# Retention followed by a low-rank mixer on one core: some of batch 1's transposes moved from TensorE to DMA, and batch 2's loads reordered

## The chip, the cores and the metric

The kernel runs on one core of a Trainium2 chip. Five engines share the work: TensorE (PE; its weight loads are listed as PEld), VectorE (DVE), ScalarE (ACT), GpSimd (POOL) and SyncE (SP), which here only issues DMA transfers. Each engine executes its own instructions in program order and waits on semaphores for the others. The metric is the device time of one execution in microseconds (us); lower is better.

## What is computed

Inputs are q, k and v of shape (4, 8, 768, 64): batch, heads, sequence, head dimension. First a linear attention with a decay per head, then a mixer on its output:

```python
gamma = 1.0 - 2.0 ** (-5.0 - np.arange(H))          # one decay per head
for t in range(S):
    state = gamma * state + k[:, :, t] (outer) v[:, :, t]
    y[:, :, t] = q[:, :, t] @ state / sqrt(D)
x = y with heads side by side                       # (4, 768, 512)
h = x.transpose(0, 2, 1) @ U @ V                    # rank 32 along the sequence
u = x + h.transpose(0, 2, 1)
out = u + relu(u @ w_ch1) @ w_ch2                   # 512 -> 2048 -> 512
```

## The kernel before, in words

The sequence of 768 is cut into six chunks of 128 (`NCK = 6`). Within a chunk the attention is two matrix products with a mask between them; between chunks a state is carried. Per chunk and batch:

- **load** (L137, or `load_heads`, L106): one 128x512 float32 tile each of k, q and v, 256 KB, issued by SyncE into a ring of 20 tiles. L137 moves rows of 64 numbers (256 bytes), L106 rows of 128 (512 bytes).
- **prep** (L207; `prep_q1` for batch 1's q): a cast or a multiplication with the decays to bf16, mostly on GpSimd, into `kd`, `qd` (called `qp` for batch 1) and `vd`. It frees a ring tile.
- **turn**: k and q are needed transposed (`kT`, `qT`). For batches 2 and 3 `turn_chunk` (L245) has SyncE issue two DMA transposes a chunk. For batch 1 `turn_k1` and `turn_q1` (L252, L261) do it on TensorE with matmuls against the identity, into a PSUM bank, and ACT or DVE copies the result out. Batch 0 has a code of its own and isn't touched.
- **score** (L276): k^T q into PSUM (matmuls of L281), then the mask (DVE, L284).
- **mix** (L289): state times query, scores times values, x copied out by ACT, the next state.

Then the low-rank part makes u (`lr_expand`, addition on DVE at L351) and its transpose `uT`. For the first four chunks of batch 1 `lr_proj_turn` and `lr_uT` make it on TensorE. The remaining u chunks go through `lr_turn` (L356): matmuls against the identity for batches 0 and 1, DMA transposes from SyncE (L359) for batches 2 and 3.

The mixer of a batch is a list of 48 pieces of nearly equal cost: 16 "up" pieces of four matmuls 128x512 (L429) on the first 512 positions, 8 "up" pieces of eight matmuls 128x256 (L442) on the other 256, and 24 "down" pieces of four matmuls (L458), four to an output row block of 128. In batch 3 the last row block is cut by columns, 384 and 128. The output is added to u on DVE (L465). It is put into a list of `stores`, from which GpSimd issues one (L408) after the next piece; only the 128-column part of the very last row block is issued by SyncE at once (L468).

**What sets the order.** The program is written out in one order, and each engine's queue follows it. `weave` (L483) goes through the 48 pieces of batch b and inserts the attention steps of batch b+1 between them. Each step has a mark, a fraction of the batch's total cost of 48 x 0.864 = 41.47; it is inserted ahead of the first piece whose accumulated cost has reached the mark. The tables `AT` and `LR` hold the marks: for batch 1 the starts of the three chunk pairs; for batches 2 and 3 the first pair's start and the distance of the pairs (`step`); then the delay of the mixes after their pair (`dm`) and the lead of the turns ahead of it (`dt`). A mark of 1.27 lies in batch 1's pieces at 0.27.

**When loads are issued.** `feed` is the list of loads in order: batch 1's by pairs, then batches 2 and 3 chunk by chunk. `feed_more` (L128) issues loads as long as fewer than `n_open` are issued and fewer than 20 ring tiles are held; each prep calls it. Before the change `n_open` is 6 * NCK = 36, so batch 2's loads follow batch 1's as ring tiles come free. `open_chunk` raises `n_open` by 3, one chunk; in batch 1's pieces six marks, 0.25 + 0.1 ci, open batch 3's chunks.

SyncE's queue is a single one: loads, DMA transposes and the last store all pass through it in program order. An instruction whose operand isn't ready holds up what stands behind it. The compiled program also makes each of its transfers wait for the eighth transfer before it. TensorE's queue is as strict: a score that waits for `kT` or `qT` holds up the mixer's matmuls behind it.

Of the kernel before, what the change touches and what calls it, by code (L numbers as in the profile page):

```python
# [10 lines left out]
bf16 = mybir.dt.bfloat16  # L11
# [5 lines left out]
def kernel(  # L17
# [11 lines left out]
    nc = tc.nc  # L29
    P = 128  # L30
    B, H, S, D = q.shape
    NCK = S // P
# [14 lines left out]
    rpre = ctx.enter_context(tc.tile_pool(name="rpre", bufs=4))  # L47
# [78 lines left out]
    n_fed, n_held, n_open = [0], [0], [6 * NCK]  # L126

    def feed_more(t=None):  # L128
        while n_fed[0] < n_open[0] and n_held[0] < RING:
            nm, b, ci = key = feed[n_fed[0]]  # L130
            n_fed[0] += 1
            n_held[0] += 1
            ready[key] = t = ring() if t is None else t
            if (nm, b) == ("q", 1):
                load_heads(t, q, 1, ci % 2, ci // 2)
            else:
                nc.sync.dma_start(  # L137
                    out=t.rearrange("p (h d) -> p h d", h=H),
                    in_=src_of[nm][b, :, ts(ci, P), :].rearrange("h p d -> p h d"))
            t = None  # L140
# [51 lines left out]
    pre = {}  # L192
# [12 lines left out]
        feed_more()  # L205

    def prep(nm, b, ci, eng="P"):  # L207
        if (nm, b) == ("q", 1):
            return prep_q1(ci)
        src = ready.pop((nm, b, ci)).rearrange("p (h d) -> p h d", h=H)  # L210
        t = rpre.tile([P, H, D], bf16, tag=nm + "d", name=f"{nm}d_{b}_{ci}")
        g = {"k": None, "q": gq, "v": gk}[nm]
        if g is not None:
            g = g[:, ci, :, None].to_broadcast([P, H, D])
        cast(eng, t, src, g)
        pre[nm, b, ci] = t
        n_held[0] -= 1
        feed_more()
# [21 lines left out]
    bts = {}  # L240

    def open_x(b):
        xs[b] = xp.tile([P, NCK, DM], bf16, tag="x", name=f"x_{b}")

    def turn_chunk(b, ci):  # L245
        for nm in "kq":
            t = bts[nm, b, ci] = rpre.tile([P, 4, P], bf16, tag=nm + "T",
                                           name=f"{nm}T_{b}_{ci}", bufs=3)
            nc.sync.dma_start(out=t, in_=pre[nm, b, ci].rearrange("p h d -> p (h d)"),
                              transpose=True)  # L250

    def turn_k1(ci):  # L252
        t = bts["k", 1, ci] = rpre.tile([P, 4, P], bf16, tag="kT", name=f"kT_1_{ci}",
# [100 lines left out]
                v4(xs[b][:, ds(j0, nj), e]), op=ALU.add)  # L354

    def lr_turn(b, j0):  # L356
        if b > 1:
            for j in (j0, j0 + 1):
                nc.sync.dma_start(out=uTs[b][:, :, ts(j, P)], in_=us[b][:, j],  # L359
                                  transpose=True)  # L360
            return
        r = R[j0 // 2 % 2]
        for c in range(NCB):
            for jj in range(2):
                nc.tensor.matmul(r[:, c // 2, ds(256 * (c % 2) + P * jj, P)],
                                 us[b][:, j0 + jj, ts(c, P)], ident, start=True,
                                 stop=True)
        evac("A", uTs[b][:, :, ds(j0 * P, 2 * P)],
             r.rearrange("p n (c t) -> p (n c) t", c=2))
# [40 lines left out]
    def mlp_pieces(b):  # L410
        gT = gtp.tile([P, NM, S], bf16, tag="gT", name=f"gT_{b}")
        pieces = []
        n = [0]

        def relu(dst, src):
            n[0] += 1
            if n[0] % 3 == 0:
                nc.vector.tensor_relu(dst, src)  # L418
            else:
                nc.scalar.activation(dst, src, AF.Relu)  # L420

        def up(m, lo, sz):
            def f():
                g_p = begun.pop((b, m, lo), None)
                c0 = 3 if g_p is not None else 0
                if not c0:
                    g_p = bank("mlp")
                for c in range(c0, NCB):
                    nc.tensor.matmul(g_p[:, :sz], w1b[:, c, ts(m, P)],  # L429
                                     uTs[b][:, c, ds(lo, sz)], start=(c == 0),  # L430
                                     stop=(c == NCB - 1))
                relu(gT[:, m, ds(lo, sz)], g_p[:, :sz])
            return f

        for m in range(NM):
            pieces.append((0.864, up(m, 0, LO)))
        def up_two(m):
            def f():
                g_p = bank("mlp")
                for n in range(2):  # L440
                    for c in range(NCB):
                        nc.tensor.matmul(g_p[:, ts(n, S - LO)], w1b[:, c, ts(m + n, P)],  # L442
                                         uTs[b][:, c, LO:], start=(c == 0),
                                         stop=(c == NCB - 1))
                relu(gT[:, ds(m, 2), LO:], g_p.rearrange("p (n t) -> p n t", n=2))
            return f

        for m in range(0, NM, 2):
            pieces.append((0.864, up_two(m)))
        hold = {}  # L450

        def down(j, m0, n0=0, nn=DM):
            def f():
                if m0 == 0:
                    hold[j, n0] = bank("mlp")
                ch = hold[j, n0]
                for m in range(m0, m0 + 4):
                    nc.tensor.matmul(ch[:, :nn], gT[:, m, ts(j, P)],  # L458
                                     w2b[:, m, ds(n0, nn)],
                                     start=(m == 0), stop=(m == NM - 1))  # L460
                if m0 == NM - 4:
                    o_sb = outp.tile([P, DM], fp32, tag="o_sb",
                                     name=f"o_{b}_{j}_{n0}")[:, :nn]
                    n = ds(n0, nn)
                    nc.vector.tensor_tensor(o_sb, ch[:, :nn], us[b][:, j, n],  # L465
                                            op=ALU.add)
                    if n0:
                        nc.sync.dma_start(out=out[b, ts(j, P), n], in_=o_sb)  # L468
                    else:
                        stores.append((nc.gpsimd, out[b, ts(j, P), n], o_sb))  # L470
            return f

        for j in range(NCK):
            if (b, j) == (B - 1, NCK - 1):
                for n0, nn in ((0, 384), (384, 128)):
                    for m0 in range(0, NM, 4):
                        pieces.append((0.864 * nn / DM, down(j, m0, n0, nn)))
                continue
            for m0 in range(0, NM, 4):
                pieces.append((0.864, down(j, m0)))  # L480
        return pieces
# [18 lines left out]
    def part(f, *args):  # L500
        return lambda: f(*args)
# [267 lines left out]
    load_w1(1024, 512)  # L769
    n_open[0] = 6  # L770
    feed_behind(511)
    n_open[0] = 6 * NCK
    load_w1(1536, 512)
    for j in range(4):
        load_w2(j)
# [3 lines left out]
    for nm in "kqv":  # L779
# [1 line left out]

    AT = {1: ((0.565, 0.685, 0.80), None, (0.045, 0.09), (0.10, 0.045), None),
          2: (0.255, 0.17, (0.05, 0.095), (0.175, 0.11),
              (0.0, 0.085, 0.17, 0.255, 0.34, 0.425)),
          3: (0.20, 0.20, (0.05, 0.095), (0.19, 0.145),
              (-0.07, 0.03, 0.13, 0.23, 0.33, 0.43))}
# [3 lines left out]
    def mark(at, f, *args):  # L792
        marks[int(at)].append((at % 1.0, part(f, *args)))
# [5 lines left out]
    for b in range(1, B):  # L799
        s0, step, dm, dt, at_prep = AT[b]  # L800
        for ci in range(NCK):
            pair_at = b - 1 + (s0[ci // 2] if b == 1 else s0 + step * (ci // 2))
            if b == 1:
                mark(pair_at - dt[0], turn_k1, ci)
                mark(pair_at - dt[1], turn_q1, ci)
            else:
                mark(b - 1 + at_prep[ci], prep_chunk, b, ci)
                mark(pair_at - dt[ci % 2], turn_chunk, b, ci)
            mark(pair_at, score, b, ci)
            mark(pair_at + dm[ci % 2], mix, b, ci)  # L810
            if b > 2:
                mark(b - 2 + 0.25 + 0.1 * ci, open_chunk)
        if b == 1:
            for nm, eng, at in (("k", "AP", (0.51, 0.635)), ("q", "PP", (0.54, 0.67)),
                                ("v", "PP", (0.58, 0.70))):
                for pp in (1, 2):
                    mark(at[pp - 1], prep_two, nm, pp, eng[pp - 1])
            mark(0.905, lr_open, b)
            mark(0.905, lr_proj_turn, b)
            mark(0.94, lr_uT, b)  # L820
            mark(1.11, lr_expand, b, 0, 4)
        else:
            l0, l1, l2, l3 = LR
            mark(b - 1 + l0, mixed, b)
            mark(b - 1 + l1, lr_expand, b, 0, 4)
            mark(b - 1 + l2, lr_turn, b, 0)
            mark(b - 1 + l3, lr_turn, b, 2)
        mark(b + 0.02, lr_expand, b, 4, 2)
        mark(b + 0.08, lr_turn, b, 4)
    mark(0.03, lr_expand, 0, 4, 2)  # L830
    mark(0.10, lr_turn, 0, 4)
    mark(0.16, lr_expand, 0, 0, 4)
# [32 lines left out]
```

## Time and profile before

| | us |
|---|---|
| median of 3 runs | 226.62 (225.92 to 226.64) |
| the profiled execution | 224.54 |
| its span (first to last instruction) | 222.7 |
| TensorE busy | 214.2 (96%) |
| VectorE busy | 96.7 (43%) |
| ScalarE busy | 82.9 (37%) |
| GpSimd busy | 80.0 (36%) |
| DMA queue of SyncE | 23.86 MB, 46.4% of 16 DMA engines' span |
| DMA queue of GpSimd | 10.42 MB, 18.3% |

The page's rows name a line of the kernel, an engine, an operation and its tiles as out<-in. A row of the chain of waits gives the start, the duration and what ran; a row of the timeline gives start, duration, engine, line, operation, tiles and count. "SPq" is SyncE's queue: the duration of its rows is the time in which the instruction holds the queue, with what it waits there; the transfer lands later, and the time from start to landing is asked for separately. In rows by windows the columns are the window and its length, busy time and instructions of PE, PEld, DVE, ACT and POOL, the clock granted to TensorE (1.00 is full), the DMA engines' busy share and GB/s.

Roughly, batch 0's attention fills 0 to 26 us, and the mixers of batches 0 to 3 run from 26 to 78, 78 to 128, 128 to 178 and 178 to 218 us.

### The profile page before, as it was taken

Reading aid. Unit: us, or ns where it says so; the run is one execution under the profiler, and the core shown is the slowest. Engines: PE = TensorE matmul, PEld = TensorE weight load, DVE = VectorE, ACT = ScalarE, POOL = GpSimd, SP = SyncE. Lnnn points to the kernel's source line nnn. Section 1 sums busy time; section 2 is a strip of 40 time slices with the busy share of each in tenths; the row PEclk is TensorE's granted clock in tenths of the full one; section 3 lists DMA queues with packets and bytes.
Section 4 is the critical chain, followed back from the end, with each engine's and each line's share of the span. In section 5 each row is a group of like instructions: output and inputs, shape, how many; then the busy total and the mean of one; then the engine's idle time right before and its main releaser. Section 6 shows DMA issues by size and latency. Waiting matters only on the chain.

```text
span 222.7 us, 4746 instructions
## 1 busy us (share of the span) xinstructions
PE 214.2 (96%) x1955; PEld 122.7 (55%) x1982; DVE 96.7 (43%) x137; ACT 82.9 (37%) x157; POOL 80.0 (36%) x115
## 2 busy tenths in 40 slices
PE   7999999999999999999999999999999999999991
PEld 2567444865665544587444444686544444864451
DVE  6678636235635346625516145251633332222111
ACT  3776454463563244565030044745120144420000
POOL 5588661125750079370101496710111100001010
PEclk9999999999999999999999999999999999999998
DMA  6999999997989996599997644411114330001211
GB/s 175 329 308 243 204 221 200 196 249 172 294 211 259 287 247 138 123 206 203 211 281 185 176 130 96 95 26 24 50 49 150 89 94 0 0 3 47 94 74 68
DMA packets 89301, 34.58 MB, mean 155 GB/s; under 512 B 71216, under 2 KB 87728, under 8 KB 89280
## 3 DMA queue, kind: packets, MB, share of 16 engines
q1 hardware_dynamic: 83152, 23.86, 46.4%
q0 software_dynamic: 6128, 10.42, 18.3%
q8 instruction: 15, 0.25, 0.5%
q14 instruction: 6, 0.05, 0.1%
HBM read 27.46 MB, written 6.29 MB: 152 GB/s over the span
## 4 chain that ended last, share of the span: by engine, by line
PE 56%; issue 31%; POOL 5%; SPq 3%; DMA 2%; DVE 1%; ACT 1%; POOLq 0%; DVEq 0%; ACTq 0%
PE mlp L458 19%; PE mlp L429 17%; PE mlp L442 6%; POOL out_dram L408 3%; SPq L106 2%; DMA in<-in_v_dram 2%; PE r L281 2%; PE r L302 1%; PE st L313 1%; PE r L297 1%; POOL vd L83 1%; PE r L639 1%; PE r L344 1%; PE r L624 1%; PE r L584 1%
## 5 line engine op out<-in xcount | busy, mean ns | idle before, releaser
L458 PE MATMUL mlp<-w2b,gT 128*128 128x512 bf16 (+2 forms) x384 | 86.6, 370 | 1.0 <-issue 0.3
L420 ACT ACTIVATE gT<-mlp 128x512 bf16<-128x512 f32 x64 | 38.1, 597 | 69.9 <-PE mlp L429 57.1
L458 PEld LDWEIGHTS <-gT 128*128 128x128 bf16 x400 | 36.9, 98 | 38.6 <-issue 0.2
L429 PE MATMUL mlp<-uT,w1b 128*128 128x512 bf16 x243 | 56.1, 379 | 0.3
L408 POOL DMA_DIRECT2D out_dram<-o x24 | 13.3, 553 | 105.0 <-DVE o L465 97.3
L418 DVE TENSOR_SCALAR gT<-mlp 128x512 bf16<-128x512 f32 x32 | 22.1, 690 | 46.2 <-PE mlp L429 23.9
L429 PEld LDWEIGHTS <-w1b 128*128 128x128 bf16 x250 | 23.6, 98 | 27.4 <-issue 0.3
L465 DVE TENSOR_TENSOR o<-mlp,u 128x512 f32<-128x512 f32 (+2 forms) x25 | 16.8, 670 | 45.1 <-PE mlp L458 44.4
L442 PE MATMUL mlp<-uT,w1b 128*128 128x256 bf16 x256 | 29.6, 273 | 0.3 <-ACT gT L420 0.2
L442 PEld LDWEIGHTS <-w1b 128*128 128x128 bf16 x256 | 24.7, 98 | 4.2 <-issue 0.4
L284 DVE TENSOR_TENSOR a<-r,mask 128x1024 bf16<-128x1024 f32 x18 | 21.2, 1219 | 7.0 <-PE r L281 7.0
L83 POOL TENSOR_TENSOR vd<-in,gk 128x512 bf16<-128x512 f32 x18 | 18.7, 1040 | 11.8 <-DMA in<-in_v_dram 11.7
L70 ACT ACTIVATE x<-r 128x512 bf16<-128x512 f32 x20 | 11.9, 596 | 26.1 <-PE r L302 25.8
L351 DVE TENSOR_TENSOR u<-r,x 128x512 bf16<-128x512 f32 (+1 forms) x16 | 14.5, 951 | 3.6 <-PE r L344 3.6
L83 POOL TENSOR_TENSOR qd<-in,gq 128x512 bf16<-128x512 f32 x12 | 12.5, 1041 | 0.0
L81 POOL CAST kd<-in 128x512 bf16<-128x512 f32 x16 | 9.7, 611 | 7.3 <-issue 6.2
L70 ACT ACTIVATE nsz<-st 64x256 bf16<-64x256 f32 x30 | 11.2, 372 | 0.3
L83 POOL TENSOR_TENSOR qp<-in,gq 128x512 bf16<-128x512 f32 x6 | 6.2, 1046 | 6.3 <-DMA in<-in_q_dram 6.3
L591 DVE TENSOR_TENSOR a<-r,mask 128x1024 bf16<-128x1024 f32 x6 | 7.3, 1222 | 2.1 <-PE r L584 2.1
L302 PE MATMUL r<-vd,a 128*128 128x64 bf16 x144 | 7.1, 193 | 0.0
L302 PEld LDWEIGHTS <-a 128*128 128x128 bf16 x144 | 6.0, 98 | 0.7
L297 PEld LDWEIGHTS <-qT 128*128 128x128 bf16 x60 | 4.6, 98 | 2.7
(109 smaller groups left out, 151.7 us busy)
## 6 DMA issues: line engine op xcount, KB each, us to landing
in<-in_k_dram SPq DMA_DIRECT2D x24, 256.0 KB, 5.0
in<-in_q_dram SPq DMA_DIRECT2D x24, 256.0 KB, 4.8
in<-in_v_dram SPq DMA_DIRECT2D x24, 256.0 KB, 4.7
out_dram<-o POOLq DMA_DIRECT2D x23, 256.0 KB, 2.5
w1b<-in_moe_w_ch_dram POOLq DMA_DIRECT2D x4, 512.0 KB, 8.1
w2b<-in_moe_w_ch_dram POOLq DMA_DIRECT2D x4, 512.0 KB, 16.1
kT<-kd SPq DMA_TRANSPOSE x12, 2.8
qT<-qd SPq DMA_TRANSPOSE x12, 2.4
```

What stands on the lines that cost most here:

```text
L70: nc.scalar.activation(dst, src, AF.Copy)
L83: e.tensor_tensor(dst, src, scale, op=ALU.mult)
L284: nc.vector.tensor_tensor(a, r.rearrange("p i (n m) -> p i n m", n=4), mask[:, None, None, :].to_broadcast([P, 2, 4, P]), op=ALU.mult)
L302: nc.tensor.matmul(o[:, ts(h, D)], a[:, i, hp], vb[:, h], start=(ci == 0 and h == 0), stop=True, skip_group_check=True)
L351: nc.vector.tensor_tensor(v4(us[b][:, ds(j0, nj), e]), R[g][:, :, :nj * P].rearrange("p c (j e) -> p c j e", j=nj), v4(xs[b][:, ds(j0, nj) ...
L408: eng.dma_start(out=dst, in_=src)
L418: nc.vector.tensor_relu(dst, src)
L420: nc.scalar.activation(dst, src, AF.Relu)
L429: nc.tensor.matmul(g_p[:, :sz], w1b[:, c, ts(m, P)], uTs[b][:, c, ds(lo, sz)], start=(c == 0), stop=(c == NCB - 1))
L442: nc.tensor.matmul(g_p[:, ts(n, S - LO)], w1b[:, c, ts(m + n, P)], uTs[b][:, c, LO:], start=(c == 0), stop=(c == NCB - 1))
L458: nc.tensor.matmul(ch[:, :nn], gT[:, m, ts(j, P)], w2b[:, m, ds(n0, nn)], start=(m == 0), stop=(m == NM - 1))
L465: nc.vector.tensor_tensor(o_sb, ch[:, :nn], us[b][:, j, n], op=ALU.add)
```

## The change

Batch 1's chunks 4 and 5 are no longer transposed by TensorE: `turn_last`, marked at 0.671 of batch 0's pieces, has SyncE issue four DMA transposes for them, k first. Their q is therefore loaded and scaled in the ordinary layout. The same goes for chunks 4 and 5 of batch 1's u: `lr_turn` uses DMA transposes for every batch but 0.

Batch 2's loads are no longer open from the beginning. At first only batch 1's are (`n_open = 3 * NCK`, 18); `turn_last` opens twelve more behind its transposes (chunks 0 to 3 of batch 2), and two `open_chunk` marks in batch 1's pieces add one chunk each.

The marks move: batch 1's last pair from 0.80 to 0.815, its low-rank steps by 0.010 to 0.015, `lr_turn` of its last chunks from 0.08 to 0.055, batch 2's first pair from 0.255 to 0.27 and the pairs' distance from 0.17 to 0.165.

Both column parts of the very last row block are stored by SyncE as soon as they are ready; all other stores go through GpSimd's list as before.

```diff
-            if (nm, b) == ("q", 1):
+            if (nm, b) == ("q", 1) and ci < NCK - 2:
                 load_heads(t, q, 1, ci % 2, ci // 2)
...
-        if (nm, b) == ("q", 1):
+        if (nm, b) == ("q", 1) and ci < NCK - 2:
             return prep_q1(ci)
...
+    def turn_dma(nm, b, ci):
+        t = bts[nm, b, ci] = rpre.tile([P, 4, P], bf16, tag=nm + "T",
+                                       name=f"{nm}T_{b}_{ci}", bufs=3)
+        nc.sync.dma_start(out=t, in_=pre[nm, b, ci].rearrange("p h d -> p (h d)"),
+                          transpose=True)
+
     def turn_chunk(b, ci):
         for nm in "kq":
-            t = bts[nm, b, ci] = rpre.tile([P, 4, P], bf16, tag=nm + "T",
-                                           name=f"{nm}T_{b}_{ci}", bufs=3)
-            nc.sync.dma_start(out=t, in_=pre[nm, b, ci].rearrange("p h d -> p (h d)"),
-                              transpose=True)
+            turn_dma(nm, b, ci)
+
+    def turn_last():
+        for nm in "kq":
+            for ci in (NCK - 2, NCK - 1):
+                turn_dma(nm, 1, ci)
+        n_open[0] = 3 * NCK + 12
+        feed_more()
...
     def lr_turn(b, j0):
-        if b > 1:
+        if b:
...
-                    if n0:
+                    if (b, j) == (B - 1, NCK - 1):
                         nc.sync.dma_start(out=out[b, ts(j, P), n], in_=o_sb)
...
-    n_open[0] = 6 * NCK
+    n_open[0] = 3 * NCK
...
-    AT = {1: ((0.565, 0.685, 0.80), None, (0.045, 0.09), (0.10, 0.045), None),
-          2: (0.255, 0.17, (0.05, 0.095), (0.175, 0.11),
+    AT = {1: ((0.565, 0.685, 0.815), None, (0.045, 0.09), (0.10, 0.045), None),
+          2: (0.27, 0.165, (0.05, 0.095), (0.175, 0.11),
...
             if b == 1:
-                mark(pair_at - dt[0], turn_k1, ci)
-                mark(pair_at - dt[1], turn_q1, ci)
+                if ci < NCK - 2:
+                    mark(pair_at - dt[0], turn_k1, ci)
+                    mark(pair_at - dt[1], turn_q1, ci)
...
+            if b == 2 and ci in (1, 3):
+                mark(pair_at - dt[1] + 0.005, open_chunk)
...
-            mark(0.905, lr_open, b)
-            mark(0.905, lr_proj_turn, b)
-            mark(0.94, lr_uT, b)
+            mark(0.671, turn_last)
+            mark(0.92, lr_open, b)
+            mark(0.92, lr_proj_turn, b)
+            mark(0.95, lr_uT, b)
...
-        mark(b + 0.08, lr_turn, b, 4)
+        mark(b + (0.055 if b == 1 else 0.08), lr_turn, b, 4)
```

## The prediction

> **What bounds the kernel now.** I read first who waits for whom with TensorE (PE) as the waiter. Each line gives waiter, releaser, total us, times, longest:
>
> ```profile
> PE mlp L753 <- DVE zeros L152: 1.2, 1, 1.2
> PE mlp L458 <- issue: 0.3, 2, 0.2
> PE mlp L442 <- ACT gT L420: 0.2, 1, 0.2
> ```
>
> After the start PE waits for nobody worth naming; the page gives it 214.2 us of a 222.7 us span. A PE instruction removed is time won, and a new PE wait is time lost, because nothing later gives it back. Next, the chain of waits (start, us, what) prices the instructions that go:
>
> ```profile
> 60.29 0.45 PE mlp L257 x8
> ...
> 64.01 0.45 PE mlp L271 x8
> ...
> 82.09 0.45 PE r L365 x8
> ```
>
> Eight 128-column transposing matmuls cost 0.45 us, 56 ns each. Then I asked what has little slack behind PE, and read SyncE's queue (SPq) in order of time around batch 2's second and third pairs:
>
> ```profile
> 93.80 1.60 SPq L249 DMA_TRANSPOSE kT<-kd  x1
> 95.50 1.21 SPq L249 DMA_TRANSPOSE qT<-qd  x1
> 96.77 0.58 SPq L137 DMA_DIRECT2D in<-in_k_dram  x1
> ...
> 104.61 1.56 SPq L249 DMA_TRANSPOSE kT<-kd  x1
> 106.28 1.20 SPq L249 DMA_TRANSPOSE qT<-qd  x1
> 107.53 0.57 SPq L137 DMA_DIRECT2D in<-in_k_dram  x1
> ...
> 112.20 0.82 SPq L137 DMA_DIRECT2D in<-in_v_dram  x1
> 113.07 1.07 SPq L137 DMA_DIRECT2D in<-in_k_dram  x1
> ```
>
> One instruction follows the next without a hole; columns are start and duration. A transpose holds this queue for 1.2 us, 1.6 right after loads. The last one of batch 2 (q of chunk 5, at 106.28) lands 2.4 us later, by the first line below (issue to landing of that instruction), so at 108.7; the second line is PE:
>
> ```profile
> DMA to landing us min/median/max: 2.4/2.4/2.4
> 108.39 0.82 PE L281 MATMUL r<-qT,kT 64*128 64x128 bf16 x16
> ```
>
> These 16 matmuls are chunks 4 and 5. They take 0.55 us in the chain's other pairs (66.86, 99.50) and here 0.82: chunk 5, from 108.8, waited for that landing. So SyncE's queue, not PE's work, already sets this point by a hair.
>
> **The change, part by part.**
>
> *Removed from PE:* two chunks' key turns (8 matmuls), their query turns (8), the last u turn (8): 24 x 56 ns = 1.35 us; 0.90 of it in batch 0's section, 0.45 early in batch 1's. The evictions that go with them (ACT 2 x 0.595, 0.747 and 1.02 us; DVE 0.734) count nothing: both engines are under 45% busy. If PE did wait for one, up to 0.2 us more is won, the size of the gaps at such places.
>
> *Marks:* a section is 48 pieces of 0.864, 41.47 in all. Batch 2's first pair moves from 0.255 x 41.47 = 10.57 to 0.27 x 41.47 = 11.20, and both fire at the piece that begins at 11.23; the other two pairs stay too (0.425 and 0.435: piece 21; 0.595 and 0.60: piece 29). So "pairs later" moves no score of batch 2; some mixes and turns go one piece later. Batch 1's last pair does move, from piece 39 to 40 (0.86 us). The two mixes and the projection behind it move with it, with the same distances between them: 0.
>
> *Batch 1's last pair:* its score comes at 66.79 - 0.90 + 0.86 = 66.75. GpSimd ends the last query multiply at 59.78 + 2.05 = 61.83, before as after (1046 against 1041 ns; chunks 4 and 5 of q now come in 256-byte rows, L137 instead of L106, perhaps 0.3 us later). The last of the four transposes can start near 63 and lands 2.4 to 4.3 us later (4.3 is the transpose at 81.86, which sat behind loads): 65.4 to 67.3. I take 0 and keep 0.6 for the range.
>
> *SyncE's queue.* The order now is: four transposes, twelve loads of batch 2, two u transposes, four transposes (chunks 0 and 1), six loads (batch 2's chunks 4 and 5, that used to be through by 81.7), four transposes (2, 3), six loads of batch 3, two transposes (4), three loads, two transposes (5). Until batch 2's last transpose the number of loads is the old one; six transposes are new. The twelve loads (63.4 to 78.4 in the trace of before) are out of SyncE's way before u is ready, at 79.50 + 1.29 - 0.90 = 79.9 (L351 on DVE). From there:
> - two u transposes, 2.5 us (120.07 to 122.62): 82.4;
> - four transposes at a pitch of 1.3 (85.75, 87.03, 88.42): 87.6. The score of chunk 1, due at 89.6, has its last operand at about 88.7: no wait;
> - six loads. The row to go by is the burst at 107.53, whose seventh load starts at 113.07: 5.54, with an output store beside it. Without a store the fourth may end when the first has landed (3.2) and two more follow at the landing pitch of 1.05, that is 5.3. I take 5.4: 93.0;
> - four transposes: 1.65 after loads, then 1.27 + 2 x 1.29 = 5.5: 98.5;
> - six loads, 5.4: 103.9;
> - two transposes, 2.9 (1.65 + 1.27): 106.8;
> - three loads, 2.2 (91.58 to 93.80): 109.0;
> - the key transpose, 1.65: the last query transpose starts at 110.7 and lands at 113.1.
>
> In the old kernel it started at 106.28, so it is 4.4 us later, while PE would like to be there 1.35 earlier. On the way chunk 3's score (due 99.72 - 1.35 = 98.4) waits until 97.2 + 2.4 = 99.6; that 1.2 is contained in the later, larger wait. Net at that point: +4.4, and the 1.35 is swallowed. Behind the waiting score all of PE stands, then the mask on DVE, the mixes, ACT's x; nothing later has a reserve to make it good.
>
> Bounds of this sum: if every load costs its bare 0.62 (91.58 to 92.20) and every transpose 1.28, the last one starts at 87.6 + 15 x 0.62 + 7 x 1.28 = 105.9, 0.4 earlier than now: -0.4, and with no wait at all -1.35. If the loads go at the crowded pitch of the stretch from 63.37 to 81.86, 15 in 18.5 or 1.23 each, 5.4 comes on top: +9.8. I stay at 4.4, because bursts of three and six from an empty queue are the nearest rows; instruction-by-instruction spread (1.2 to 1.8 for a transpose) gives it about 1.2 either way.
>
> The Trainium skill ("DMA: Bandwidth & Descriptors", Latency and other measured facts) gives a DMA transpose 261 GB/s. By that, as an estimate, one of 128 KB takes 0.5 us and the six new ones 3 us; the rows say 1.28 us of queue each, 7.7, and the measurement decides.
>
> *Last row's store:* the 384-column part goes from GpSimd (218.19) to SyncE, free then, right after DVE's 217.90; its issue (0.37) is over before the last part's at 218.55, whose landing (2.0) ends the run as before: 0. If the two collided, 0.4.
>
> *Removing the early loads of batch 2* wins nothing: the stretch from 48 to 78.3 is DMA-full, but PE is busy 29.88 of 30.30 us in it.
>
> **Sum:** +4.4 on the profiled execution, 224.54 (span 222.7) to 228.9. The runs shown have a median of 226.62, 2.1 above it, and the same difference puts it at **231.0**.
>
> **The rivals.**
> 1. *The wait also costs clock.* The granted clock (the column of 1.00, 0.86, 0.50) after the last matmul, which ends at 218.2:
>
> ```profile
> 220.50:221.00 0.50, 0.00 (x0) 0.00 (x0) 0.00 (x0) 0.00 (x0) 0.00 (x0) 1.00 0.00 0
> 221.00:221.50 0.50, 0.00 (x0) 0.00 (x0) 0.00 (x0) 0.00 (x0) 0.00 (x0) 0.86 0.00 0
> 221.50:222.00 0.50, 0.00 (x0) 0.00 (x0) 0.00 (x0) 0.00 (x0) 0.00 (x0) 0.50 0.00 0
> ```
>
> PE falls to half speed some 3.2 us after its last work. The wait at chunk 5 would be about 113.1 - 108.7 = 4.4, longer than that. If half speed then lasts as long as it took to come, 1.6 us are lost: 232.6. Against it: it depends on when the idle time began against the clock's own beat. The Trainium skill ("TensorE: Matmul & The Clock Gate", The HAM clock gate) says so: a free-running window of 3.4 us, throttled after an idle one; as an estimate by it the price is up to 1.7 us, and this rule speaks against the change. No row shows a return from half speed in mid-kernel.
>
> 2. *The queue keeps up (the other side).* SyncE hides fifteen loads behind the matmuls at 0.62 us each, and the 24 matmuls are the whole story: 226.62 - 1.35 = 225.3. It decides as soon as the last query transpose starts before 107.5 - 2.4 = 105.1. For it: PE is the bound on every view of the page. Against it: the third load of every burst already takes 0.87 to 1.45, not 0.57.
>
> 3. *Batch 1's last pair is late as well,* by 0.6: u is later, and the whole queue with it: 231.6; with an instruction or two at the long end 232.5.
>
> 4. *It doesn't matter:* queue and gain cancel, a wait of 1.35: 226.6. It needs the queue 4 us faster than summed.
>
> **How the numbers follow.** Likeliest case 0.52 (231.0, its own range 229.8 to 232.3); rival 1 0.23; rival 3 0.10; rival 2 0.08; rival 4 0.07. The range leaves out rivals 2 and 4 (0.15) and the far ends: 228.2 to 233.9. A difference under 0.3% (0.7 us) can't be told from none here. Faster 0.08, same 0.06, slower 0.86.
>
> **What would show it.** Right: SyncE's transposes of batch 2's chunk 5 start 4 us later than 104.61 and 106.28; PE has one gap of about 4 us before L291 (the score's line after the change) near 109, a smaller one ten us earlier, and everything behind is shifted by it; 24 fewer transposing matmuls. Wrong: no such gap, or the largest one in batch 1's last pair; the prediction as a whole is wrong if a burst of six loads takes SyncE under 4 us.

## The result, and the profile after

| | before | after |
|---|---|---|
| median of the runs taken together | 225.94 (225.13 to 226.64, 6 runs) | 234.42 (231.12 to 237.24, 6 runs) |
| the profiled execution | 224.54 | 231.12 |
| its span | 222.7 | 229.4 |
| last matmul to the end of the span | 4.5 | 3.0 |

The changed kernel is slower: the ratio is 1.031, with an interval from 1.025 to 1.037. On the 226.62 us from which the forecast started that is 233.6. The traced execution is the fastest of the six, 231.12; the trace explains its 6.6 us over the traced execution of before, and what that leaves open stands ahead of the lessons. The ratios, here and below, leave disturbed runs out; the medians don't.

Who waits for whom, with TensorE as the waiter (us in total, times, longest). The first and the third line are new; the third is a wait at 52.28 us, in batch 1's first pair:

```profile
PE r L291 <- DMA qT<-qd: 5.5, 2, 3.3
PE mlp L763 <- DVE zeros L152: 1.2, 1, 1.2
PE r L291 <- ACT qT L70: 0.5, 1, 0.5
```

L291 is the score (L281 before; lines after it are ten higher). Two scores wait for transposed queries, 5.5 us together. The timeline of TensorE shows which (start, us, line, operation, count; in brackets the idle time before it and what ended it):

```profile
98.86 0.40 PE L291 MATMUL r<-qT,kT 64*128 64x128 bf16 x8
101.44 0.54 PE L291 MATMUL r<-qT,kT 64*128 64x128 bf16 x8 [2.18 <-DMA qT<-qd]
101.91 4.27 PE L452 MATMUL mlp<-uT,w1b 128*128 128x256 bf16 x24
...
109.11 2.75 PE L468 MATMUL mlp<-w2b,gT 128*128 128x512 bf16 x12
111.80 0.40 PE L291 MATMUL r<-qT,kT 64*128 64x128 bf16 x8
115.50 0.61 PE L291 MATMUL r<-qT,kT 64*128 64x128 bf16 x8 [3.31 <-DMA qT<-qd]
116.05 4.02 PE L468 MATMUL mlp<-w2b,gT 128*128 128x512 bf16 x12
```

Eight matmuls are one chunk. Batch 2's chunk 2 scores at once and chunk 3 waits 2.18 us; ten us later chunk 4 scores at once and chunk 5 waits 3.31. The third and the last line show something more: 24 matmuls 128x256 take 4.27 us and 12 matmuls 128x512 take 4.02; the same 12 at 109.11, between the two waits, take 2.75. The same execution by windows (length, busy time and instructions of PE, PEld, DVE, ACT and POOL, then the granted clock, DMA share, GB/s) gives the reason:

```profile
100.00:101.00 1.00, 0.00 (x0) 0.00 (x0) 0.80 (x1) 0.00 (x0) 0.00 (x0) 1.00 0.58 131
...
101.50:102.00 0.50, 0.50 (x9) 0.30 (x10) 0.00 (x0) 0.00 (x0) 0.00 (x0) 0.57 0.53 125
102.00:103.00 1.00, 1.00 (x6) 0.69 (x7) 0.91 (x1) 0.00 (x0) 0.00 (x0) 0.50 1.20 271
...
104.00:105.00 1.00, 1.00 (x7) 0.73 (x5) 0.00 (x0) 0.44 (x1) 0.00 (x0) 0.51 1.19 270
105.00:106.00 1.00, 1.00 (x11) 0.90 (x10) 0.00 (x0) 0.60 (x1) 0.00 (x0) 1.00 1.13 256
...
115.50:116.00 0.50, 0.50 (x8) 0.35 (x8) 0.00 (x0) 0.00 (x0) 0.00 (x0) 0.50 0.95 218
116.00:117.00 1.00, 1.00 (x6) 0.41 (x4) 0.78 (x1) 0.00 (x0) 0.00 (x0) 0.50 1.22 276
...
119.00:120.00 1.00, 1.00 (x7) 0.48 (x6) 0.00 (x0) 0.00 (x0) 0.00 (x0) 1.00 1.13 256
```

After each wait the granted clock, the number behind the five busy times, is 0.50 for some three us. And SyncE's queue, which makes the operands (start, time for which the instruction holds the queue):

```profile
79.61 0.84 SPq L137 DMA_DIRECT2D in<-in_v_dram  x1
80.70 2.91 SPq L369 DMA_TRANSPOSE uT<-u  x2
...
88.95 0.58 SPq L137 DMA_DIRECT2D in<-in_k_dram  x1
...
94.42 1.86 SPq L248 DMA_TRANSPOSE kT<-kd  x1
...
98.98 1.22 SPq L248 DMA_TRANSPOSE qT<-qd  x1
100.25 0.57 SPq L137 DMA_DIRECT2D in<-in_k_dram  x1
...
105.49 1.48 SPq L248 DMA_TRANSPOSE kT<-kd  x1
...
112.46 1.24 SPq L248 DMA_TRANSPOSE qT<-qd  x1
```

The last of these is chunk 5's query. It lands 2.91 us after its start, at 115.37, and the score begins at 115.50; chunk 3's, from 98.98, lands at 101.31, and its score begins at 101.44. Both waits end with SyncE's queue, which has no hole of more than 0.5 us between 80.70 and there.

Where the time went, from DVE's instructions that both traces have (after less before, us): -0.12 when batch 1's section starts; -0.57 after the last u turn; -0.57 still at batch 2's third chunk; +3.40 behind chunk 3's wait and the half clock; +6.69 at chunk 5's score (TensorE's rows, 115.50 and 108.81); +8.17 after the second half clock, and the same up to the last matmul (226.36 against 218.20). From there to the end of the span it is 1.54 us less than before: 8.17 - 1.54 = 6.63, the difference of the two spans.

### The profile page after: what moved, and what is told of

It is laid out like the page before. It is cut to its first block, busy times and chain, and to the rows that moved or that the text cites. A ratio compares the mean times of both kernels' runs of the same rounds, so it can differ in the third digit from the quotient of the medians.

```text
span 229.4 us, 4714 instructions
## 1 busy us (share of the span) xinstructions
PE 218.2 (95%) x1958; PEld 122.7 (53%) x1958; DVE 96.3 (42%) x136; ACT 80.1 (35%) x153; POOL 79.5 (35%) x114
## 4 chain that ended last, share of the span: by engine, by line
PE 57%; DMA 16%; issue 9%; SPq 8%; POOL 7%; DVE 1%; ACT 1%; POOLq 0%; DVEq 0%
PE mlp L468 28%; PE mlp L439 12%; DMA in<-in_q_dram 8%; PE mlp L452 6%; SPq L137 5%; DMA in<-in_k_dram 5%; DMA w1b<-in_moe_w_ch_dram 3%; SPq L248 3%; POOL vd L83 2%; PE mlp L763 2%; POOL qd L83 2%; DMA qT<-qd 1%; PE r L291 1%; POOL kd L81 1%; DVE a L601 1%
## 5 line engine op out<-in xcount | busy, mean ns | idle before, releaser
L468 PE MATMUL mlp<-w2b,gT 128*128 128x512 bf16 (+2 forms) x400 | 89.0, 375 | 0.0
L418 POOL DMA_DIRECT2D out_dram<-o x23 | 12.7, 554 | 110.8 <-DVE o L475 110.8
L439 PEld LDWEIGHTS <-w1b 128*128 128x128 bf16 x250 | 23.6, 98 | 28.0 <-issue 0.3
L452 PE MATMUL mlp<-uT,w1b 128*128 128x256 bf16 x256 | 30.9, 281 | 0.2 <-ACT gT L430 0.2
L452 PEld LDWEIGHTS <-w1b 128*128 128x128 bf16 x256 | 25.5, 101 | 4.8 <-issue 0.6
L83 POOL TENSOR_TENSOR qd<-in,gq 128x512 bf16<-128x512 f32 x14 | 14.5, 1042 | 0.0
L291 PE MATMUL r<-qT,kT 64*128 64x128 bf16 x144 | 6.5, 225 | 6.0 <-DMA qT<-qd 5.5
L291 PEld LDWEIGHTS <-kT 64*128 64x128 bf16 x144 | 4.4, 96 | 9.8 <-issue 9.7
L83 POOL TENSOR_TENSOR qp<-in,gq 128x512 bf16<-128x512 f32 x4 | 4.2, 1048 | 8.0 <-DMA in<-in_q_dram 8.0
```

The lines of the kernel that those rows point to most:

```text
L83: e.tensor_tensor(dst, src, scale, op=ALU.mult)
L291: nc.tensor.matmul(r[:, i, ts(hp, P)], kT[ri, hp], qT[ri, hp], start=True, stop=True)
L418: eng.dma_start(out=dst, in_=src)
L439: nc.tensor.matmul(g_p[:, :sz], w1b[:, c, ts(m, P)], uTs[b][:, c, ds(lo, sz)], start=(c == 0), stop=(c == NCB - 1))
L468: nc.tensor.matmul(ch[:, :nn], gT[:, m, ts(j, P)], w2b[:, m, ds(n0, nn)], start=(m == 0), stop=(m == NM - 1))
```

## The experiments

Each time stands beside the kernel before, run on the same chip in the same round; "before" differs a little from chip to chip, so the ratios are what to compare. The theory under test: SyncE's queue, longer by six transposes, makes two scores late; each wait of more than two us also costs half clock; and the store at the end gains by itself.

**1. The store alone**, in the kernel before:

```diff
-                    if n0:
+                    if (b, j) == (B - 1, NCK - 1):
```

> The kernel before with one part of the change alone: both column parts of the last row block stored by SyncE. In the changed kernel the span ends 3.0 us after the last matmul, before it was 4.5. Theory (GpSimd's closing instruction, 3.5 us long, begins behind its last store, and without that store it begins 2.5 us earlier): the run ends about 1.5 us earlier, 224.4 against 225.9, with PE's work unchanged. The rival is the prediction's step, that the last landing decides and the move costs and gains nothing: 225.9, the difference at the end coming from something else in the changed kernel.

Measured: 223.51 us (10 runs) against 225.38, ratio 0.9915 (0.988 to 0.995). Last matmul to span's end: 3.1 us, where it was 4.5. The chain that ended last (start, us, what), of before:

```profile
212.28 0.54 POOL out_dram L408
212.81 2.90 issue
215.73 0.54 POOL out_dram L408
216.27 1.90 issue
218.17 0.56 POOLq L860
```

and of this run:

```profile
208.76 9.71 PE mlp L458 x60
218.50 0.29 DVE o L465
```

Before, the run's end hangs on GpSimd: its last store goes out at 218.19, and its closing instruction (L860, the end of the program) holds its sequencer from 218.17 to 221.73; the engines' common end comes after that. Here GpSimd has its last store 2.2 us sooner, its closing instruction lasts from 215.97 to 219.54, and what comes last is SyncE's second store, landed at 220.46, with the span's end at 221.60. So the store is a gain of about 1.5 us in the trace, 1.9 in the times, and it is in the changed kernel too.

**2. The u transposes alone**, in the kernel before:

```diff
-        if b > 1:
+        if b:
```

> The kernel before with one part of the change alone: the last u chunks of batch 1 turned by two DMA transposes, nothing else (loads open as before, the last two chunks of batch 1 turned by TensorE, last store by GpSimd). Theory (SyncE's queue had no reserve at batch 2's chunk 5): two more transposes of 1.28 us put its last operand 2.6 us later, PE comes 0.45 earlier and waits about 3; net 2.6 us longer, 1.5 more if the clock halves: 228.0 to 229.5 where the old kernel takes 225.4. Rival (the queue has room for two, it takes all six and the reordered loads to be late): 225.0, a little faster.

Measured: 228.92 to 230.67 us in three executions, ratio 1.017 (1.0135 to 1.021). The fourth, the traced one, took 771.22 us, with matmuls of L458 at 1065 ns instead of 370; it can't be compared, and so no trace shows where the three lost their time. Two transposes more in SyncE's queue, and 0.45 us of matmuls less, cost some 4 us: the loss doesn't need the moved loads or marks.

**3. Batch 3's loads later**, in the changed kernel. Ahead of the transposes of chunks 2 and 3 there stand then three loads and not six, ahead of chunk 4's three and not six, ahead of chunk 5's none and not three:

```diff
-                mark(b - 2 + 0.25 + 0.1 * ci, open_chunk)
+                mark(b - 2 + 0.50 + 0.045 * ci, open_chunk)
```

> The changed kernel, but batch 3's chunks are opened from 0.50 of batch 1's pieces in steps of 0.045 instead of 0.25 in steps of 0.1. Twelve loads less stand ahead of batch 2's last transposes in SyncE's queue (nine of batch 3, and three of batch 2's chunk 5, which the second step now opens behind the transposes of chunks 2 and 3). Theory (order of SyncE's queue makes both waits): no wait at the scores of chunks 3 and 5, no half clock; PE ends 0.6 to 1.4 us before the old kernel and the end is 1.5 shorter: 223.0 to 223.8 where the old kernel takes 225.9. Rival (the transposes themselves are slow because loads run beside them in the DMA engines, whose number per batch is unchanged): waits of 1 to 3 us remain, 229 or more.

Measured: 231.77 us, ratio 1.027 (1.020 to 1.034). The timeline of TensorE:

```profile
99.32 0.62 PE L291 MATMUL r<-qT,kT 64*128 64x128 bf16 x16
99.87 2.79 PE L452 MATMUL mlp<-uT,w1b 128*128 128x256 bf16 x24
...
133.98 1.87 PE L439 MATMUL mlp<-uT,w1b 128*128 128x512 bf16 x4 [6.45 <-DMA uT<-u]
```

Both waits are gone (sixteen matmuls in a row), and the 24 matmuls take 2.79 us at full clock, not 4.27. The rival (loads slow the transposes from beside them) expected waits of 1 to 3 us to remain at these scores, and there are none. Until 127.6 us TensorE is 0.1 to 0.3 ahead of before, less than the 0.6 to 1.4 that was expected. Then comes a wait of 6.45 that was not foreseen: eighteen loads in a row, from 106.32 to 126.6, hold back batch 2's u transposes, and the clock is at half from 130.11 to 136.94. The waits at the scores were the queue's order; moving the loads in one block moved the wait. The total said nothing; the trace did.

**4. Chunk 5's loads ahead only**: experiment 3, with both of batch 2's late chunks opened in the first step.

```diff
-            if b == 2 and ci in (1, 3):
+            if b == 2 and ci < 2:
```

> As e2_batch3_later, batch 3's loads late, but both remaining chunks of batch 2 are opened together, ahead of the transposes of chunks 2 and 3, as they stand in the changed kernel. It parts the two waits. Theory: the six loads of batch 2 make the wait at chunk 3 (2.3 us, and 1.7 for half speed), batch 3's nine make the one at chunk 5. So the first stays and the second goes: 225.9 - 0.6 + 4.0 - 1.5 = 227.8. Rival (batch 3's loads make both, by filling the DMA engines): as e2_batch3_later, 223 to 224.

Measured: 233.99 us, ratio 1.0375 (1.029 to 1.046). Its timeline:

```profile
102.73 0.61 PE L291 MATMUL r<-qT,kT 64*128 64x128 bf16 x8 [2.24 <-DMA qT<-qd]
...
137.42 1.86 PE L439 MATMUL mlp<-uT,w1b 128*128 128x512 bf16 x4 [5.25 <-DMA uT<-u]
```

Chunk 3 waits 2.24 us, with half clock from 102.41 to 105.82, and TensorE goes from 0.3 to 4.5 us behind; chunk 5 doesn't wait and stays there. So the two waits are separate and each goes with the loads ahead of it. The u wait is that of experiment 3 again, and for it the total misses the 227.8 that was expected.

**5 and 6. TensorE kept busy through the waits**, to price the half clock by itself: matmuls on zeros ahead of batch 2's chunk 3 and chunk 5 scores, 9 and 14, then 10 and 22.

```diff
+        for _ in range({(2, 3): 9, (2, 5): 14}.get((b, ci), 0)):
+            nc.tensor.matmul(r[:, 0], zeros[:, :P], zeros, start=True, stop=True)
```

> The changed kernel with matmuls of zeros ahead of two scores of batch 2, 9 before chunk 3's (1.9 us) and 14 before chunk 5's (3.0 us), which only fill the waits of 2.3 and 3.3 us; the scores overwrite what they write. Theory (the waits' second price is the clock: two windows of 3.4 us at half speed cost 1.7 and 1.5): no window at 0.50 before the end, 3.2 us less than the changed kernel, about 230.5 where that takes 233.7. Rival (half speed is only recorded, or costs little because the operands are the limit): same time as the changed kernel, within 1 us.

> As e3_kept_busy, whose second wait was longer than its fill (14 matmuls of zeros, then 2.1 us idle and half clock): now 10 ahead of chunk 3's score (2.2 us) and 22 ahead of chunk 5's (4.7 us). In e3 the first wait passed without half clock. Theory: if the fill covers both waits there is no window at 0.50 before the end and PE's delay is that of the landings alone: 226.9 + 3 to 5, about 230 to 231 where the old kernel takes 225.4. Rival (half speed costs nothing): 232 to 234 as the changed kernel, and no gain from the fill.

Measured: 232.72 us, ratio 1.031 (1.023 to 1.038), and 233.57, ratio 1.035 (1.030 to 1.040). In the first, chunk 3's wait fell to 0.7 and no half clock followed; chunk 5's operand came 1.7 us later than in the changed kernel, a wait of 2.09 was left and half clock after it, from 117.99 to 121.40. In the second no window is below 1.00, and still nothing was won: its last query transpose of batch 2 started at 116.64 instead of 112.46, though the same loads and transposes stand in the same order. Its own rows show where: the first transpose behind loads held the queue for 2.88 us (1.86 in the changed kernel), the next such one for 2.87 (1.48). Part of that was late from the start: TensorE was 1.9 us behind by 48 us, ahead of every changed instruction. So the clock follows the wait, as the theory has it, but these runs don't give a net price. The price stays with the rows: 4.27 against 2.79 for 24 matmuls, 4.02 against 2.75 for 12, and the score itself 0.61 against 0.40.

**7. Batch 3's loads spread** over the holes of SyncE's queue, in the changed kernel:

```diff
-                mark(b - 2 + 0.25 + 0.1 * ci, open_chunk)
+                mark(b - 2 + (0.50, 0.545, 0.59, 0.90, 1.085, 1.13)[ci], open_chunk)
```

> The changed kernel with batch 3's chunks opened at 0.50, 0.545 and 0.59 of batch 1's pieces (behind batch 2's last transposes), the fourth at 0.90 (behind the first u transposes of batch 2), the last two at 0.085 and 0.13 of batch 2's pieces. In e2_batch3_later the waits at chunks 3 and 5 were gone (PE 0.3 us ahead of the old kernel at 127 us), but eighteen loads in a row then held up batch 2's u transposes, a wait of 6.4 us and 6.8 us of half clock. Theory (it is only the order in SyncE's queue): no wait over 1 us anywhere; PE ends 0.3 to 1.3 us before the old kernel, the end is 1.5 shorter: 222.6 to 223.6 where the old kernel takes 225.4. Rival (six transposes more than the queue can hold, however they are ordered): a wait of 3 us or more appears in batch 2's up pieces or batch 3's scores, 227 or more.

Measured: 226.69 us (12 runs) against 225.59, ratio 1.004 (1.001 to 1.007). TensorE's waits:

```profile
PE r L291 <- DMA qT<-qd: 2.0, 3, 1.7
PE mlp L763 <- DVE zeros L152: 1.2, 1, 1.2
```

No wait in batch 2's scores or its u; from 84 us on TensorE is 0.1 to 0.5 us ahead of before until 147 us. Then batch 3's chunk 3 waits 1.69 and the last pair after it more, 1.54 behind before in all, and the end, 3.4 us after the last matmul, gives 1.1 back. Nearly the whole loss was the order of the queue: 1.031 becomes 1.004 with the same six new transposes. But the gain didn't come out.

**8. One chunk earlier**: the last three marks of experiment 7 are 0.61, 0.90 and 1.085.

```diff
-                mark(b - 2 + (0.50, 0.545, 0.59, 0.90, 1.085, 1.13)[ci], open_chunk)
+                mark(b - 2 + (0.50, 0.545, 0.59, 0.61, 0.90, 1.085)[ci], open_chunk)
```

> The changed kernel with batch 3's six chunks opened at 0.50, 0.545, 0.59, 0.61, 0.90 and 1.085 of batch 1's pieces: against the run that spread them (225 to 227 us), the fourth, fifth and sixth chunk come one step earlier, three of the loads into the hole of SyncE's queue at 117.25 to 119.7 us of that run. Theory (the loss is only the order of SyncE's queue): the new waits at batch 3's scores (0.61 at its chunk 3, 1.54 from its second pair on) shrink to under 0.6 in all, no wait comes at batch 2's scores or its u, the last matmul ends 0.3 us or more ahead of the kernel before's, and with 1.5 us at the end the run is 1.5 to 2 us faster than before, about 223.7 us; level with the run that changes the store alone (223.5). Rival (six more transposes can't find room in this queue wherever the loads are put): the three loads move the wait to batch 2's u transposes, some 1 to 2 us, and the run stays level with before, 225 to 227 us.

Measured: 225.43 us (12 runs) against 227.13 on this chip, ratio 0.995 (0.991 to 0.9985). The waits at batch 3's scores are gone. In their place twelve loads end at 121.0, 0.2 us behind u (ready at 120.82); the first u transpose starts at 121.09 and holds the queue for 2.08 us, where it took 1.20 in experiment 7, and TensorE loses 0.76 there. That is the rival's mechanism, at a smaller price than it named. By the ratio the run is faster than before, as the theory said, but by some 1.1 us and not 1.5 to 2; whether it is level with the store alone the two intervals, which overlap, can't tell. Its one trace doesn't show the gain (span 223.2 against 222.7): TensorE was 0.8 us behind there by 48 us, ahead of every changed instruction.

**9. The same, with batch 1's u turned by TensorE**:

```diff
         if b:
...
+        if b > 1:
```

> The same order of loads, and batch 1's last two u chunks transposed by TensorE again (8 matmuls, 0.45 us): SyncE has 4 new transposes and not 6, 2.5 us less of queue ahead of batch 2's scores. Theory: no wait at all at batch 2's and batch 3's scores but for what is left of those at batch 3's pair 2 (under 0.5), the last matmul ends 0.2 to 0.5 us ahead of before's, 223.5 to 224 us, within 0.5 us of the same order with the u transposes on SyncE. Rival (there is no room for any of them): waits of 1 us or more stay, and the run is level with before.

Measured: 224.16 us (10 runs) against 227.13, ratio 0.990 (0.987 to 0.994). TensorE's waits by name, and its timeline where a score waits:

```profile
PE st L615 <- POOL vu L83: 1.6, 1, 1.6
PE mlp L763 <- DVE zeros L152: 1.2, 1, 1.2
PE r L291 <- DMA qT<-qd: 0.7, 1, 0.7
```

```profile
69.81 0.40 PE L291 MATMUL r<-qT,kT 64*128 64x128 bf16 x8 [0.72 <-DMA qT<-qd]
```

Nothing waits in batches 2 and 3. (The 1.6 us is in batch 0, at 17 us, in code that the change doesn't touch, and no other trace has as much there.) What is left is batch 1's last pair, whose DMA transposes come 0.72 late: TensorE is 1.93 us behind before at 48 us, and again 1.93 when batch 1's mixer begins, so the 0.90 us of matmuls that went are all eaten there. From 48 us to the last matmul this kernel wins 0.2 us by the trace, and at the end 1.0. Its ratio, 0.990, can't be told from the 0.9915 of the store alone. Against experiment 8 the medians are 1.3 us apart, where 0.5 or less was expected, but these two intervals overlap as well.

## Why the prediction was right, and where it was off

**Right in sign, place and mechanism.** PE's two new gaps are at batch 2's chunks 3 and 5, the larger at chunk 5, the smaller 14 us ahead of it (ten were predicted); everything behind stays shifted. The score's operand is late because SyncE's queue is: chunk 5's transposes start at 110.90 and 112.46, over 6 us later than before, where 4 was the sign. Experiment 3 takes loads out of the queue's way and both gaps go, 4 takes one, 2 makes a loss, by its times alone, without any of the rest.

**The queue's sum, 2.3 us too small.** Start of each step, as worked out and as in the trace:

| | predicted | trace | late by |
|---|---|---|---|
| two u transposes | 79.9 | 80.70 | 0.8 |
| four transposes end, six loads start | 87.6 | 88.95 | 1.35 |
| four transposes | 93.0 | 94.42 | 1.4 |
| six loads | 98.5 | 100.25 | 1.75 |
| two transposes | 103.9 | 105.49 | 1.6 |
| three loads | 106.8 | 108.34 | 1.55 |
| last query transpose | 110.7 | 112.46 | 1.75 |
| it lands | 113.1 | 115.37 | 2.3 |

More than half of it was there before the first burst, and it begins with u. The first u transpose starts at 80.70, right behind DVE's two additions that make u:

```profile
79.38 1.29 DVE L361 TENSOR_TENSOR u<-r,x 128x512 bf16<-128x512 f32 x2 [0.47 <-PE r L354]
```

They end at 80.67 and not at 79.9, because of the 0.90 us that batch 0's section was to win only 0.12 had come (0.59 was lost at batch 1's first pair and 0.2 at its last, see below). The twelfth load holds the queue until 80.45, so even a u at 79.9 would have waited: the step that has the twelve loads "out of SyncE's way before u is ready" failed too. The first u transpose behind them held the queue for 1.60, not for half of 2.5.

Behind that the bursts of six were priced well, 5.47 and 5.24 (5.4), and so were two transposes, 2.85 (2.9). The second four transposes took 5.83, not 5.5: the first, right behind loads, took 1.97 to the next start where 1.65 was the row (1.59 and 1.56 behind the later loads). The three loads took 2.56, not 2.2, and the last transpose landed after 2.91 us, not 2.4, with loads around it. Chunk 3's operand landed at 101.31, not at 99.6, and its wait was 2.18, not 1.2.

**Rival 1 came true as well.** It had 0.23; it should have had more. Two waits brought two stretches at 0.50. The first is contained in the second wait, as the prediction says of the wait itself, since the queue and not TensorE sets chunk 5's landing; the second costs 1.48 (12 matmuls 1.27, the score 0.21), where 1.6 was worked out. The prediction leaned on an idle time over 3.2 us; the first wait, 2.2, was enough. The Trainium skill ("TensorE: Matmul & The Clock Gate", The HAM clock gate) speaks of a free-running window of about 3.4 us. The trace agrees with the window: half clock lasts 3.41 us both times, and the two stretches begin 13.65 us apart, four times that. It doesn't agree that a whole idle window is needed: the 3.41 us ahead of the first stretch, from 98.16 to 101.57, hold 2.18 us of idle time and 1.2 us of matmuls.

**The last row's store was priced at 0 and is worth 1.5.** The step read the end by the landing of the last part. The chain of waits of before ended on GpSimd's sequencer, behind its last store, and that was on the page to be read; what lies between the last landing and the span's end was never asked.

**Removed from PE, 1.35.** The u turn gave its 0.45 at once (-0.12 to -0.57). The last pair's 0.90 came short, by two things. The first pair's score, which the change leaves alone, waited 0.53 at 52.28 for an ACT eviction that stood behind a load, and 0.59 was lost; none of the other traces has this wait. And at the last pair the fourth transpose landed at 67.62, with the score begun at 67.35, which cost 0.2 us; the prediction had 65.4 to 67.3 for this landing and took a wait of 0. That is rival 3's mechanism, at 0.2 us and not 0.6; in experiments 3, 4, 8 and 9 the same place waits 0.65 to 1.26. For TensorE the 1.35 is swallowed at chunk 3, as predicted; but through u what was missing of it made the queue later, as rival 3 said.

**Marks.** Batch 2's pairs did not move: -0.57 at chunk 0 and at chunk 2.

On the traced execution: 4.4 expected; 2.27 more of queue, 1.48 of clock, 1.54 less at the end make 6.6, as measured. That the forecast missed by the queue's 2.3 alone is luck: a loss left out of the sum (the clock) and a gain priced at 0 (the store) cancelled each other.

**What stays open.** The six runs of the changed kernel spread over 6 us, before's over 1.5, and only the fastest was traced; the forecast's offset of 2.1 us between trace and median was 3.3 here. In experiment 6, with the same order in the queue, the last query transpose starts 4.2 us later and lands 3.7 us later, so the queue's own spread can do a part of it. The mean granted clock on record, in the order of the times, is 0.985, 0.983, 0.985, 0.977, 0.977 and 0.970; two stretches of half clock, as in the trace, make 0.985 (3.41 of 229.4 us lost). No trace of a slower run was taken, so where the others lost more isn't shown. Nor is it shown why a transpose behind loads holds the queue for 1.5 us in one run and 2.9 in another.

## What to carry to other kernels

Work moved from a busy engine to a DMA queue is priced at the queue, instruction by instruction with everything that stands ahead of it: 0.45 us of matmuls became some 2.5 us of queue, by the rows of before, and cost 4 us (experiment 2). Where a queue carries loads and transposes together, first ask which loads stand ahead of the transpose that someone waits for; here the order alone was worth 1.031 against 1.004. And read the end of the run by itself: no kernel of this case beats, beyond its interval, the old one with one store on another queue.

## What the hardware showed that I had not expected

- GpSimd's closing instruction takes 3.5 us behind its last store (218.17 to 221.73 before, 215.97 to 219.54 in experiment 1, 224.16 to 227.66 after), and in none of the traces does the run end before it: before, the span's end comes 1.0 us behind it. Moving one store to SyncE won 1.4 us of span after the last matmul in experiment 1, 1.5 in the changed kernel.
- A wait of TensorE of 2.1 to 2.2 us was enough for half clock (2.18 after, 2.24 in experiment 4, 2.09 in experiment 5); waits of 1.69 (experiment 7) and below brought none. It lasts 3.41 us, twice that after the 6.45 us of experiment 3 and the 5.25 of experiment 4, on a beat that is the same through one execution. With TensorE's time cut into windows of 3.41 us on that beat, each of the seven windows between the first full clock and the last matmul with 2.09 us or more of idle time was followed by half clock (two in the changed kernel, two in experiment 3, two in 4, one in 5). Of the windows at full clock with 1.65 us or less none was.
- Half clock has its cost only if nothing later catches it: chunk 3's 1.7 us vanish in chunk 5's wait.
